# A linear-attention and top-2 mixture-of-experts kernel: ScalarE issues the stores of the rows of x and the early slot fetches, and copies those rows before the logits are summed

## The chip, the cores and the metric

The kernel runs on one core of a Trainium2 chip. The metric is the device time of one execution in microseconds (us). Before the change the median of three runs is 662.22 us (660.88 to 662.79). Below, PE is TensorE's matmul, PEld its weight load, DVE is VectorE, ACT is ScalarE, POOL is GpSimd and SP is SyncE; a q behind a name (SPq) means the engine's sequencer, which waits and issues transfers.

## The reference

```python
# attention: B, H, S, D = 4, 8, 768, 48
f = 1.0 / (1.0 + np.exp(-f_logit))
for t in range(S):
    state = f[:, :, t, :, None] * state + np.einsum('bhd,bhe->bhde', k[:, :, t], v[:, :, t])
    y[:, :, t] = np.einsum('bhd,bhde->bhe', q[:, :, t], state)
# bridge: x = y as rows, (B*S, H*D) = (3072, 384)
# router: E = 8 experts, F = 1024
logits = x @ w_gate
noisy_logits = logits + np.log1p(np.exp(x @ w_noise)) * noise
top2 = np.argpartition(-noisy_logits, 2, axis=1)[:, :2]      # and top2_w: softmax over the two
for e in range(E):
    for k in range(2):
        mask = top2[:, k] == e
        h = np.maximum(x[mask] @ w1[e], 0.0)
        out[mask] += top2_w[mask, k, None] * (h @ w2[e])
```

All of it is float32.

## The kernel before

The sequence is cut into chunks of 128 steps; with 6 chunk positions and 4 batches there are 24 (position, batch) chunks, numbered n = 4c + b. A loop over i runs seven stages, each on another chunk, so that the chunks are pipelined: `forget` on n = i+3 (transposes f, takes its logarithm, line 545 on), `scaled` on i+1 (transposes q and k and scales them on VectorE: qP line 566, kQ line 568), `scores` on i (score matrix, line 580, masked into A, line 583; below the last position also a copy kn on ScalarE, line 576), `summed` on i+2 (running sum L on VectorE, line 554), `output` on i-1 (y, lines 598 and 609, copied to yT on ScalarE, line 613), `decays` on i+2 (P, Q and far on ScalarE, lines 559 to 562) and `features` on i-2. `features` multiplies yT by `w_rt` (line 633), which yields in one PSUM bank the 384 columns of x's rows and the columns of the logits. VectorE sums the logits (`lg`, line 636), then ScalarE copies the rows to `xs` (line 638), and a closure is put in the list `xw` that stores `xs` to `x_rows` in DRAM (line 639). The list is emptied in the next turn of the loop, after the `scaled` stage, that is behind the `forget` instructions of that turn.

PSUM tiles of one bank come from a pool of six banks in rotation, so a bank is written again by the sixth tile after it: the transposes of k in a turn reuse the bank that yT was copied from in the turn before.

After the last chunk of a position, `route` picks two experts for each token, in small pieces between the stages, and queues 8 `puts` (line 710): indirect transfers from POOL that write each token's entry into its expert's list in DRAM (`lists`). Experts are worked on in `items`. The first four items, the early experts, take the first 256 entries of their lists and can start once the first three positions (`HALF`) are routed; their first part is woven into the end of the attention by `first_loads`. Such an item begins with `fetch` (line 815), which reads 256 list entries to `slots`; then `gather` (line 826) on POOL reads the rows of x that the slots name from `x_rows` to `xg`, in two halves; `turned` (line 862) transposes them on TensorE, and the two layers follow (`first_layer`, line 914; `second_layer`, line 1021). Before the change SP issues all plain transfers: the loads of f, q, k and v (line 528), the stores of x, the zeros of out (line 1254), the weights (lines 834 to 844) and the fetches.

Each engine keeps the order in which the program was traced (`in_order`). A transfer is thus issued when its engine comes to it in that order and its semaphores have been reached. In the program as built, the transfers of SP signal their landing on eight semaphores in turn, and each first waits for the transfer that used its semaphore before, the eighth ahead of it.

Of the kernel before, what the change touches and what calls it, by code (L numbers as in the profile page):

```python
# [15 lines left out]
AX = mybir.AxisListType  # L16
ALU = mybir.AluOpType
# [314 lines left out]
def kernel(  # L332
# [38 lines left out]
    nc = tc.nc  # L371
# [4 lines left out]
    C = 128  # L376
# [10 lines left out]
    NE = 4  # L387
# [33 lines left out]
    def one_bank(name):  # L421
        turns.append(turns.pop(0))
        return turns[-1].tile([128, 512], F32, tag="one", name=name)
# [51 lines left out]
    x_rows = tc.dram_tile([N, DM], F32, name="x_rows")  # L475
    lists = tc.dram_tile([LR, 4], U32, name="lists")
# [9 lines left out]
    XW = 2 * D  # L486
# [29 lines left out]
    xw, puts, n_put = [], [], []  # L516
    logf, L, P, Q, qP, kQ, A, kn, yT, lg = ({} for _ in range(10))
# [4 lines left out]
    def cols(hp):  # L522
        return slice(hp * C, (hp + 1) * C)
# [105 lines left out]
    def features(n):  # L629
        c, b = n // B, n % B  # L630
        xp = one_bank(f"xp_{n}")[:, 0:HP * (XW + 2 * E)].rearrange("t (a w) -> t a w", a=HP)
        for hp in range(HP):
            nc.tensor.matmul(xp[:, hp, :], lhsT=yT[n][:, hp % 2, cols(hp // 2)], rhs=w_rt[:, hp, :], start=True, stop=True)  # L633
        if b == 0:
            lg[c] = rt.tile([128, B, 2 * E], F32, tag="lg", name=f"lg_{c}", bufs=NCH)
        nc.vector.tensor_reduce(lg[c][:, b, :], xp[:, :, XW:].rearrange("t a e -> t e a"), axis=AX.X, op=ALU.add)
        xs = wk.tile([128, HP, XW], F32, tag="xs", name=f"xs_{n}", bufs=3)
        nc.scalar.copy(xs, xp[:, :, 0:XW])
        xw.append(lambda: nc.sync.dma_start(out=x_rows[n * C:(n + 1) * C, :], in_=xs.rearrange("t a w -> t (a w)")))


    def route(c):
# [137 lines left out]
    slots, xg, xt, hcol = {}, {}, {}, {}  # L780
# [29 lines left out]
    def fetch(p):  # L810

        assert len(n_put) >= (HALF if p < NE else NCH) * B * 2
        slots[p] = ffn.tile([128, 2, 4], U32, tag=f"slots{p < NE}", name=f"slots{p}", bufs=8)
        row = pairs[p][0] * N + pairs[p][1]
        got = nc.sync.dma_start(out=slots[p], in_=lists[row:row + 256, :].rearrange("(s p) w -> p s w", p=128))
        if p < NE:

            tc.declare_no_dep(got.ins, group="later", reason="slots differ")
            tc.add_to_no_dep_group("full", got.ins)
# [47 lines left out]
    def ahead(what, until):  # L867
        if what in (1, 2):
            most = len(items) if what == 1 else done[1]
        else:  # L870
            most = min(NP if len(n_put) == NCH * B * 2 else NE, NP if what == "fetch" else done["fetch"])
        while done[what] < min(until, most):
            t = done[what]
            done[what] += 1
            fetch(t) if what == "fetch" else gather(t) if what == "gather" else weights(t, what)
# [408 lines left out]
    pieces = chain.from_iterable(((k, i) for i, _ in enumerate(first_layer(k) if k < NE else first_of_two(k))) for k in range(len(items)))  # L1284
    for i in range(-3, NS + 2):
        for stage, lag in ((forget, -3), (scaled, -1), (scores, 0), (summed, -2), (output, 1), (decays, -2), (features, 2)):
            n = i - lag
            if not 0 <= n < NS:
# [26 lines left out]
            for when, first_n, last_n, whose, layer, part in ((output, 13, 16, 0, 1, 0), (output, 17, 18, 0, 2, 0),  # L1315
                                                              (features, 16, 17, 0, 2, 2), (features, 20, 23, 1, 1, 0)):
                if stage is when and first_n <= n <= last_n:
                    part_of_weights(whose, layer, part + n - first_n)
# [14 lines left out]
        n = i - 2  # L1333
        if n >= 0 and n % B == B - 1:
            c = n // B
# [25 lines left out]
    for item, piece in pieces:  # L1361
        p = first_of[item] + max(0, piece - 8) // 7 if item >= NE else item
# [5 lines left out]
        n = item - NE - 2  # L1368
# [52 lines left out]
```

## Time and profile before

| what | value |
|---|---|
| median of 3 runs | 662.22 us |
| the profiled execution's own time | 667.17 us |
| its span on the core | 665.4 us |
| mean granted TensorE clock | 0.985 |
| PE busy | 637.2 us, 96% |
| PEld busy | 550.1 us, 83% |
| DVE busy | 441.8 us, 66% |
| POOL busy | 266.9 us, 40% |
| ACT busy | 254.6 us, 38% |

The profiled execution took 1.77 us more than its span, and 4.95 us more than the median of the unprofiled runs. The times of instructions below are counted from the span's start. Attention takes about the first 170 us, the experts the rest. Matmuls are pipelined and their ends are modelled.

### The profile page before, as it was taken

Reading aid. Unit: us, or ns where it says so; the run is one execution under the profiler, and the core shown is the slowest. Engines: PE = TensorE matmul, PEld = TensorE weight load, DVE = VectorE, ACT = ScalarE, POOL = GpSimd, SP = SyncE. Lnnn points to the kernel's source line nnn. Section 1 sums busy time; section 2 is a strip of 40 time slices with the busy share of each in tenths; the row PEclk is TensorE's granted clock in tenths of the full one; section 3 lists DMA queues with packets and bytes.
Section 4 is the critical chain, followed back from the end, with each engine's and each line's share of the span. In section 5 each row is a group of like instructions: output and inputs, shape, how many; then the busy total and the mean of one; then the engine's idle time right before and its main releaser. Section 6 shows DMA issues by size and latency. Waiting matters only on the chain.

```text
span 665.4 us, 12898 instructions
## 1 busy us (share of the span) xinstructions
PE 637.2 (96%) x4883; PEld 550.1 (83%) x4883; DVE 441.8 (66%) x993; ACT 254.6 (38%) x603; POOL 266.9 (40%) x300
## 2 busy tenths in 40 slices
PE   7999999967999999999999999999999999999991
PEld 7999988856999998999858965995698579889891
DVE  7777867853457666787666676757576667766751
ACT  5876766731221233333233333333322332232320
POOL 7633888715077623261521450325034214413021
PEclk9999999997999999999999999999999999999997
DMA  9999887893599423465725760836184337602112
GB/s 183 190 220 230 187 168 150 186 250 101 168 330 224 106 47 69 118 184 201 222 86 170 170 167 25 292 46 189 26 288 97 91 116 211 180 3 25 22 25 29
DMA packets 153897, 96.31 MB, mean 145 GB/s; under 512 B 115600, under 2 KB 146320, under 8 KB 153824
## 3 DMA queue, kind: packets, MB, share of 16 engines
q1 hardware_dynamic: 141648, 76.12, 41.6%
q0 software_dynamic: 12176, 19.25, 15.3%
q8 instruction: 41, 0.67, 0.4%
q14 instruction: 32, 0.26, 0.1%
HBM read 75.97 MB, written 19.62 MB: 144 GB/s over the span
## 4 chain that ended last, share of the span: by engine, by line
PE 93%; DMA 3%; issue 1%; DVE 1%; POOL 0%; SPq 0%; ACT 0%; POOLq 0%; DVEq 0%
PE y L1021 32%; PE P L939 8%; PE hp L914 6%; PE W L939 5%; PE Z L939 5%; PE V L939 5%; PE X L939 5%; PE xp L633 4%; PE sc L580 4%; PE y L598 4%; PE xgp L862 2%; PE y L609 2%; PE kp L540 2%; PE fp L540 1%; PE qp L540 1%; PE ds L604 1%
## 5 line engine op out<-in xcount | busy, mean ns | idle before, releaser
L1030 POOL DMA_INDIRECT out_dram<-ys,slots x48 | 81.8, 1705 | 154.1 <-ACT ys L1088 131.8
L1021 PE MATMUL y<-qk_all,f_all 128*128 128x192 f32 x576 | 105.2, 327 | 0.0
L1021 PEld LDWEIGHTS y<-qk_all,f_all 128*128 128x128 f32 x576 | 93.3, 190 | 0.3 <-DVE f_all L1003 0.3
L826 POOL DMA_INDIRECT xg<-x_rows,slots x48 | 53.5, 1114 | 50.5 <-DMA slots<-lists 34.1
L1021 PE MATMUL y<-w,hs_b 128*128 128x192 f32 x320 | 59.1, 328 | 0.0
L710 POOL DMA_INDIRECT lists<-entry,sloti x48 | 52.0, 1083 | 10.3 <-issue 9.9
L1021 PEld LDWEIGHTS y<-w,hs_b 128*128 128x128 f32 x320 | 52.9, 190 | 0.9
L1162 POOL DMA_INDIRECT out_dram<-ys_q,slots_q x5 | 8.6, 1718 | 104.0 <-DVE ys_q L1160 104.0
L914 PE MATMUL hp<-xt_a,w 128*128 128x256 f32 x192 | 43.7, 383 | 0.0
L975 ACT ACTIVATE hs_b<-hs_b 128x256 f32<-128x256 f32 (+1 forms) x32 | 15.1, 472 | 71.7 <-DVE hs_b L955 68.4
L914 PEld LDWEIGHTS hp<-xt_a,w 128*128 128x128 f32 x192 | 35.8, 190 | 4.9 <-issue 0.3
L939 PE MATMUL X<-xt_a,w 128*128 128x256 f32 (+1 forms) x128 | 39.7, 432 | 0.0
L939 PE MATMUL Z<-xt_b,v_all 128*128 128x256 f32 (+1 forms) x128 | 39.7, 432 | 0.0
L583 DVE TENSOR_TENSOR A<-sc,causal 128x1024 f32<-128x1024 f32 x24 | 29.3, 1222 | 13.4 <-PE sc L580 7.3
L1088 ACT ACTIVATE ys<-ys,slots 128x384 f32<-128x384 f32 x24 | 14.8, 617 | 59.7 <-DVE ys L1087 49.5
L1080 DVE TENSOR_TENSOR ys<-P,y 128x192 f32<-128x192 f32 x24 | 8.5, 354 | 42.2 <-PE y L1021 29.0
L955 DVE TENSOR_TENSOR hs_b<-hs_a,X 128x256 f32<-128x256 f32 (+1 forms) x32 | 15.6, 487 | 29.9 <-PE X L939 29.8
L1021 PE MATMUL y<-w,f_all 128*128 128x192 f32 x192 | 35.1, 326 | 0.0
L862 PE MATMUL xgp<-ident,xg 128*128 128x128 f32 x144 | 24.3, 279 | 9.9 <-DMA xg<-x_rows,slots 9.9
L939 PEld LDWEIGHTS X<-xt_a,w 128*128 128x128 f32 x128 | 24.3, 190 | 10.1
L939 PEld LDWEIGHTS Z<-xt_b,v_all 128*128 128x128 f32 x128 | 24.3, 190 | 10.1
L955 DVE TENSOR_TENSOR hs_a<-hs_a,P 128x256 f32<-128x256 f32 (+1 forms) x64 | 31.1, 486 | 1.4
(199 smaller groups left out, 1445.1 us busy)
## 6 DMA issues: line engine op xcount, KB each, us to landing
w<-in_moe_w_dram SPq DMA_DIRECT2D x16, 1536.0 KB
w_q<-in_moe_w_dram SPq DMA_DIRECT2D x10, 1536.0 KB
w<-in_moe_w_dram SPq DMA_DIRECT2D x16, 384.0 KB
f_all<-in_f_logit_dram SPq DMA_DIRECT2D x24, 192.0 KB
qk_all<-in_q_dram SPq DMA_DIRECT2D x24, 192.0 KB
qk_all<-in_k_dram SPq DMA_DIRECT2D x24, 192.0 KB
v_all<-in_v_dram SPq DMA_DIRECT2D x24, 192.0 KB
x_rows<-xs SPq DMA_DIRECT2D x24, 192.0 KB
```

The source lines that it names most:

```text
L540: nc.tensor.transpose(p[:, cols(hp)], flat[:, cols(hp)], ident)
L580: nc.tensor.matmul(sc[:, par, cols(hp)], lhsT=kQ[n][rows(par), cols(hp)], rhs=qP[n][rows(par), cols(hp)], start=True, stop=True)
L583: nc.vector.tensor_tensor(A[n].rearrange("j r (a i) -> j (r a) i", i=C), sc.rearrange("j r (a i) -> j (r a) i", i=C), causal.unsqueeze(1). ...
L598: nc.tensor.matmul(at(hp, par), lhsT=vt[:, 2 * hp + par, :], rhs=A[n][:, par, cols(hp)], start=(hp < 2), stop=(c == 0 and hp >= HP - 2))
L710: into = nc.gpsimd.indirect_dma_start(out=lists, out_offset=bass.IndirectOffsetOnAxis(ap=sloti[:, r, b:b + 1], axis=0), in_=entry[:, c, b, ...
L826: nc.gpsimd.indirect_dma_start(out=xg[p][:, s, :], out_offset=None, in_=x_rows[0:HALF * B * C] if p < NE else x_rows, in_offset=bass.Indir ...
L862: nc.tensor.transpose(xp[:, i * 128:(i + 1) * 128], xg[p][:, s, i * 128:(i + 1) * 128], ident)
L914: nc.tensor.matmul(hp[:, o, :], lhsT=w1[home(k)][:, i, (fo + o) * 128:(fo + o + 1) * 128], rhs=xt_a[:, i, k % 2 * 256:(k % 2 + 1) * 256], ...
L939: nc.tensor.matmul(to, lhsT=x, rhs=y, start=start, stop=stop)
L955: nc.vector.tensor_tensor(to, x, y, ALU.add)
L1021: nc.tensor.matmul(P[name], lhsT=x[:, o, :], rhs=y[:, o, :], start=(o == 0), stop=(o == FH - 1))
L1030: into = nc.gpsimd.indirect_dma_start(out=out, out_offset=bass.IndirectOffsetOnAxis(ap=slots[p][:, s, 2:3], axis=0), in_=ys[s], in_offset= ...
```

## The change

Three edits. In `features` the copy of the rows on ScalarE is traced before VectorE's sum of the logits, which reads the same bank. The store of the rows is issued by ScalarE instead of SP. And for the four early items (`p < NE`) the fetch of the slots is issued by ScalarE, not SP.

```diff
@@ features
         if b == 0:
             lg[c] = rt.tile([128, B, 2 * E], F32, tag="lg", name=f"lg_{c}", bufs=NCH)
-        nc.vector.tensor_reduce(lg[c][:, b, :], xp[:, :, XW:].rearrange("t a e -> t e a"), axis=AX.X, op=ALU.add)
         xs = wk.tile([128, HP, XW], F32, tag="xs", name=f"xs_{n}", bufs=3)
         nc.scalar.copy(xs, xp[:, :, 0:XW])
-        xw.append(lambda: nc.sync.dma_start(out=x_rows[n * C:(n + 1) * C, :], in_=xs.rearrange("t a w -> t (a w)")))
+        nc.vector.tensor_reduce(lg[c][:, b, :], xp[:, :, XW:].rearrange("t a e -> t e a"), axis=AX.X, op=ALU.add)
+        xw.append(lambda: nc.scalar.dma_start(out=x_rows[n * C:(n + 1) * C, :], in_=xs.rearrange("t a w -> t (a w)")))
@@ fetch
-        got = nc.sync.dma_start(out=slots[p], in_=lists[row:row + 256, :].rearrange("(s p) w -> p s w", p=128))
+        got = (nc.scalar if p < NE else nc.sync).dma_start(out=slots[p], in_=lists[row:row + 256, :].rearrange("(s p) w -> p s w", p=128))
```

## The prediction

> **What bounds the kernel now.** I read the page first, then TensorE's waits, the chain in order of time, the windows around TensorE's one long wait, and the timelines of SP and ScalarE ahead of it. The page:
>
> ```profile
> PE 637.2 (96%) x4883; PEld 550.1 (83%) x4883; DVE 441.8 (66%) x993; ACT 254.6 (38%) x603; POOL 266.9 (40%) x300
> ...
> PE 93%; DMA 3%; issue 1%; DVE 1%; POOL 0%; SPq 0%; ACT 0%; POOLq 0%; DVEq 0%
> ```
>
> TensorE is the bound: 93% of the chain is its own work, which this change leaves alone. Only the 3% of DMA can be won. TensorE's waits (engine line <- releaser: us in total, times, longest):
>
> ```profile
> PE xgp L862 <- DMA xg<-x_rows,slots: 9.9, 1, 9.9
> PE fp L540 <- DVE f_all L534: 1.8, 2, 1.0
> ```
>
> The chain where it leaves TensorE (start, us, what):
>
> ```profile
> 141.04 1.10 PE sc L580 x16
> 142.23 4.89 DMA slots<-lists
> 147.93 4.85 DMA xg<-x_rows,slots
> 154.50 1.68 PE xp L633 x8
> ```
>
> There is one wait worth naming. TensorE finishes `output` of chunk 21 at 143.75 and goes on at 153.63, when the first gather is there; the gather waited for the slots, whose fetch SP issued only at 142.23. The windows (stretch; width, busy us of PE, PEld, DVE, ACT, POOL; granted clock, DMA share, GB/s) show what follows:
>
> ```profile
> 144.00:150.00 6.00, 0.00 (x0) 0.00 (x0) 0.00 (x0) 0.43 (x2) 1.76 (x2) 0.82 1.06 311
> 150.00:156.00 6.00, 2.37 (x12) 2.40 (x13) 0.56 (x1) 0.00 (x0) 4.81 (x10) 0.50 0.54 159
> 156.00:162.00 6.00, 6.00 (x44) 4.92 (x44) 1.18 (x5) 0.48 (x1) 3.82 (x6) 0.83 0.48 103
> ```
>
> The clock is halved from 147.78, 4.03 after the wait began, to 158.02, 4.39 after it ended. Why was the fetch late? SP's timeline, then ScalarE's:
>
> ```profile
> 135.66 2.23 SPq L639 DMA_DIRECT2D x_rows<-xs  x1
> 137.95 0.43 SPq L528 DMA_DIRECT2D v_all<-in_v_dram  x1
> 138.43 2.73 SPq L844 DMA_DIRECT2D w<-in_moe_w_dram  x2
> 141.25 0.41 SPq L639 DMA_DIRECT2D x_rows<-xs  x1
> ...
> 142.23 0.88 SPq L815 DMA_DIRECT2D slots<-lists  x1
> ```
>
> ```profile
> 130.83 0.50 ACT L638 COPY xs<-xp 128x384 f32<-128x384 f32 x1
> ...
> 132.53 0.20 ACT L549 COPY cap<-f 128x4 f32<-128x4 f32 x1
> 134.46 0.65 ACT L613 COPY yT<-y 128x256 f32<-128x256 f32 x2 [1.73 <-PE y L609]
> ```
>
> SP runs late: the store issued at 141.25 is of chunk 17, whose rows were copied at 130.83. In the order of tracing that store and the fetch stand right behind the `cap` that ends at 132.73, ahead of yT. The last put of the first half was issued by 129.63, so the lists are no hindrance.
>
> **The fetch on ScalarE.** ScalarE reaches it at 132.73, but may not issue it then. The eight landing semaphores are, I take it, dealt over SP's and ScalarE's transfers together, so each waits for the eighth ahead of it. The landings, which the views do not print, I read from the semaphores' updates in the same trace. The store of chunk 17 would wait for the weights issued at 130.25, landed 136.95; the fetch for the q issued at 131.96, landed 138.74. It is then issued at about 138.8, or 3.43 earlier than 142.23. Its flight: 4.89 in the row above; the second fetch (144.18) landed at 147.77, 3.59 later. I take the middle, 4.24, as ScalarE's transfers queue behind fewer of their kind: 0.65 won, ends 0 and 1.3. Then as before 0.81 to the gather, 4.85 flight and 0.85 to the matmul: 138.8 + 4.24 + 0.81 + 4.85 + 0.85 = 149.55 instead of 153.63, 4.08 won. POOL, which does the state of chunk 19 ahead of the gather, is done by about 141.7 then (yT at 139.3, the copy of ds and POOL's 0.73 and 0.62 behind it), so it does not hold it. The other three early fetches lead to gathers that no matmul waited for: 0.
>
> "DMA: Bandwidth & Descriptors" of the Trainium skill (Issuing engines are not separate DMA queues) speaks against more: transfers share the same DMA engines whoever starts them, and a second issuer saves only the time to initiate. By it the flight stays 4.89 and the sum is 3.43; by the row of the second fetch it is 4.73.
>
> **The stores on ScalarE.** SP loses 24 issues; the row of x_rows has their range in ns (least, median, most), and ScalarE's waits have the room for them:
>
> ```profile
> L639 SPq DMA_DIRECT2D x_rows<-xs x24: 319/754/2616, 31.2 to 177.8; - x24
> ```
>
> ```profile
> ACT yT L613 <- PE y L609: 24.9, 17, 2.2
> ```
>
> No ScalarE issue is in the trace. Bounds are 0.32 and 2.62 us; I take the median 0.75, from the same transfer. It cannot be negative, as ScalarE issued nothing before. It stands ahead of kn and yT; behind it all of ScalarE's queue waits (kn, yT, ds, P, Q, far, xs), and for yT TensorE does: yT's second copy ended at 129.54, and the transposes of k that reuse such banks began at 129.98, 0.44 later. ScalarE idles 24.9/17 = 1.46 before yT, so 0.75 is covered, up to 1.46 + 0.44 = 1.90 a chunk. Without that cover the first 18 stores would cost 13.5 us.
>
> The semaphore wait comes on top. For chunks 0 to 12, the eighth transfer ahead landed between 2.86 before and 0.74 after ScalarE came by: covered but for tenths. Chunk 13 is different: ScalarE comes at 107.38, the q issued at 103.52 landed at 112.74, a hold of 5.36. With SP's 0.67 issue of that store, less its own idle 1.68 and 0.44, TensorE gets 3.9 late. Chunks 14, 16 and 17 would be held 4.2 to 4.3, but by then all is 3.9 late, so little comes on top. If the dealing is shifted by one (the k that landed at 114.50), it is 5.6; if SP, relieved of 10.6 us of issue for the stores of chunks 9 to 16, gets its loads landed sooner, it is 0. I take 3.9, the row as it stands. It is nothing at the end while it hides in the wait: TensorE comes to the gather at 143.75 + 3.9 = 147.65, at most 149.35, still before 149.55.
>
> **The rows ahead of the sum.** ScalarE waited for the sum 13.1 us in three waits, 12.05 of them inside TensorE's wait, so 0 is won. Now the sum waits for the copy: for chunk 17 from 129.97 to 131.33, 1.36 later. Behind it on VectorE stand qP (130.38), kQ (130.99), A (131.83) and L. qP moves to about 131.5, 1.1 later; TensorE needs kQ at 136.30 and A (over at 133.06) at 137.40, 4.3 of slack, and the bank of the sum at 132.27, against 131.58 then. Worth 0; where VectorE is full (5.76 of 6 us in 120 to 126) the slack takes the delay. Without it 1.1 a chunk.
>
> **The clock.** TensorE's gap shrinks from 9.9 to 149.55 - 147.65 = 1.9. That is under half of the 4.03 after which the clock fell, so the half-clock stretch of 4.39 goes: at most 2.2 won. But the second half of the gather was issued 2.64 behind the first (150.57, 147.93), and is waited for instead. From the first transposes to the first matmuls of the item (153.63 to 158.44) it took 4.81; now 2.64 + 0.49 for the transposes + 1.09 for the scores = 4.2. Won 0.6, ends 0 and 2.2.
>
> "TensorE: Matmul & The Clock Gate" (Part 1) puts the idle time that halves the clock at about 3.4 us; the trace's gap had lasted 4.03. A new gap between the two would keep this loss by the page, not by the row; mine is under both.
>
> **Sum.** 4.08 + 0.6 = 4.7. From 158 on TensorE is full, and the later loads follow its progress (SP's weights wait 153.7 for W and 121.7 for y), so it stays. The profiled execution's 667.17 becomes 662.5; off the median of 662.22, 4.95 below it, the same gain gives 657.5.
>
> **The rivals.**
>
> *The stall goes altogether.* SP without the stores lands its loads sooner, ScalarE is held by nothing, and the fetch is issued near 133.5. TensorE would be stopped only by its own arrival at 143.75: 9.9 + 0.6 = 10.5 at most, 651.7; halfway, 654. For it: SP's issues are nearly back to back. Against: transfers issued near 131 took 7 us to land, which is not SP's issuing.
>
> *ScalarE becomes the bound of the attention (slower).* Each store holds ScalarE, by issue and semaphore, ahead of yT, and TensorE waits in each chunk. The price is the hold above 1.90; it decides once the lateness of 18 chunks passes 10.5, that is 0.58 a chunk, a mean hold of 2.48. SP's longest issue, 2.62, gives 18 x 0.72 = 13.0, so 2.5 slower: 664.7; with 3.9 more for chunk 13, 668.6. For it: issues of 1.39 to 2.62 for chunks 14 to 16, holds over 4. Against: the median of 0.75, and chunks 0 to 12.
>
> *The fetch is no earlier.* ScalarE, itself late behind stores, comes to it at 142. Then only tenths move: 660.5 to 663.
>
> **How the numbers follow.** Forecast 0.45 (655.5 to 660), the stall gone 0.15, the fetch no earlier 0.12, ScalarE the bound 0.28. About 0.3%, 2 us, is what a measurement of this kernel tells from no change. Faster 0.60 (the first two), same 0.12, slower 0.28. The range leaves out the best of the second case, under 653, and the worst of the last, above 668. The forecast's own range is 655.5 to 660.
>
> **What would show it.** Right: the fetch issued by ScalarE near 139 landing by 143.5; TensorE's wait for xg under 3 us; no half clock after 145; a wait of ScalarE for a DMA before store 13, with yT late and TensorE held some 4 us near 110. Wrong: xp's spacing above 6.5 us from the start (ScalarE binds), a fetch at 133 (stall gone) or after 142, or VectorE's qP late enough that scores wait for it.

## The result

The changed kernel takes 661.92 us (median of 12 runs, 659.16 to 665.33); the kernel before, timed beside it, 661.50 us (12 runs, 658.75 to 662.79). The ratio is 1.0009 [0.9989, 1.0030]: no difference that the measurement can tell. 657.5 and "faster" were forecast. In the comparisons below the medians are of all runs, and the ratio leaves out runs over 1.5% above the fastest of their own kernel: one each in e10 and e11, three each in e6 and e13, and six of 12 in e9, its profiled execution among them.

The profiled execution of the changed kernel seems to tell another story: 662.21 us of its own (span 660.5), 4.96 less than the profiled execution of before, and almost the 662.5 forecast for it. The page after:

```profile
PE 637.2 (96%) x4883; PEld 550.0 (83%) x4883; DVE 441.6 (67%) x993; ACT 254.8 (39%) x603; POOL 271.7 (41%) x300
...
q10 hardware_dynamic: 4544, 4.74, 2.0%
...
PE 87%; DMA 5%; DVE 2%; POOL 1%; ACT 1%; issue 1%; SPq 1%; ACTq 0%; POOLq 0%; DVEq 0%
...
L638 DVE TENSOR_REDUCE lg<-xp 128x16 f32<-128x64 f32 x24 | 5.3, 222 | 42.6 <-ACT xs L637 42.6
```

TensorE's own work is the same 637.2 us, and q10 is ScalarE's new queue. But the chain has lost 6 points of TensorE: it now runs through DMA, VectorE, POOL and ScalarE. Before the sum of the logits VectorE now idles 42.6 us, all of it for the copy xs. TensorE's waits after:

```profile
PE xgp L862 <- DVE sp L658: 1.9, 1, 1.9
...
PE qp L540 <- ACT kn L576: 1.7, 3, 1.0
...
PE y L598 <- ACT yT L613: 0.9, 1, 0.9
```

Of the wait of 9.9 us for the first gather 1.9 is left. The view names VectorE for it, whose `sp` ended at 150.62; but the semaphore for which TensorE's queue had waited just before is that of the gather's second half, which landed at 150.61. Small waits for ScalarE stand where there were none. The windows after (columns as in the prediction):

```profile
144.00:150.00 6.00, 4.24 (x59) 3.53 (x59) 4.26 (x7) 3.21 (x10) 4.93 (x7) 1.00 0.40 100
150.00:156.00 6.00, 5.26 (x29) 4.48 (x30) 4.18 (x13) 0.00 (x0) 4.72 (x9) 0.72 0.26 39
```

TensorE is busy in the stretch that was empty, and the clock is halved for 3.4 us (151.23 to 154.65) instead of 10.2. What it was paid with is in ScalarE's timeline and in the chain in order of time:

```profile
133.64 0.20 ACT L549 COPY cap<-f 128x4 f32<-128x4 f32 x1
138.47 0.33 ACTq L639 DMA_DIRECT2D x_rows<-xs  x1
139.03 0.42 ACTq L815 DMA_DIRECT2D slots<-lists  x1
139.49 0.65 ACT L613 COPY yT<-y 128x256 f32<-128x256 f32 x2 [5.66 <-PE sc L580]
```

```profile
130.65 8.30 DMA out_dram<-zero
...
139.03 0.42 ACTq L815
...
139.49 0.20 ACT yT L613
```

ScalarE stands from 133.84 to 138.47 ahead of the store of chunk 17, and then at the fetch until a zeroing of the output, issued by SP at 130.65, has landed. Nothing in the data asks the fetch to wait for that: the zeroing is the transfer that used the fetch's landing semaphore before. The data alone would not have let it go much sooner here, though: by its semaphore's updates the last put that the fetch reads landed at 138.23. Behind the fetch stands yT, on which the chain goes on. The two profiles are not a fair pair, though: the 667.17 of before lies above all 12 of its runs, the 662.21 of after amid its own. In the runs nothing was won, and the experiments had to show why.

### The profile page after: what moved, and what is told of

It reads as the page before. It is cut to its first block, busy times and chain, and to the rows that moved or that the text cites. A ratio compares the mean times of both kernels' runs of the same rounds, so it can differ in the third digit from the quotient of the medians.

```text
span 660.5 us, 12835 instructions
## 1 busy us (share of the span) xinstructions
PE 637.2 (96%) x4883; PEld 550.0 (83%) x4883; DVE 441.6 (67%) x993; ACT 254.8 (39%) x603; POOL 271.7 (41%) x300
## 4 chain that ended last, share of the span: by engine, by line
PE 87%; DMA 5%; DVE 2%; POOL 1%; ACT 1%; issue 1%; SPq 1%; ACTq 0%; POOLq 0%; DVEq 0%
PE y L1021 32%; PE P L939 8%; PE hp L914 7%; PE X L939 5%; PE V L939 5%; PE Z L939 5%; PE W L939 5%; PE sc L580 3%; PE y L598 3%; PE xp L633 3%; PE xgp L862 2%; DMA f_all<-in_f_logit_dram 1%; DMA out_dram<-zero 1%; PE y L609 1%; PE qp L540 1%; DMA w<-in_moe_w_dram 1%
## 5 line engine op out<-in xcount | busy, mean ns | idle before, releaser
L710 POOL DMA_INDIRECT lists<-entry,sloti x48 | 54.2, 1129 | 11.9 <-issue 9.5
L638 DVE TENSOR_REDUCE lg<-xp 128x16 f32<-128x64 f32 x24 | 5.3, 222 | 42.6 <-ACT xs L637 42.6
L1021 PEld LDWEIGHTS y<-w,f_all 128*128 128x128 f32 x192 | 31.9, 190 | 0.0
```

Source lines behind the costliest of these rows:

```text
L710: into = nc.gpsimd.indirect_dma_start(out=lists, out_offset=bass.IndirectOffsetOnAxis(ap=sloti[:, r, b:b + 1], axis=0), in_=entry[:, c, b, ...
L1021: nc.tensor.matmul(P[name], lhsT=x[:, o, :], rhs=y[:, o, :], start=(o == 0), stop=(o == FH - 1))
```

## The experiments

**Theory H**: the wait for the first gather is real, and the earlier fetch wins what it should; but ScalarE, which now issues transfers, is held at each until an older transfer on the same landing semaphore has landed, and everything behind it (kn, yT, P, Q, xs) is late by that. **Rivals**: the wait of the first profile was an unusual one (A); issuing itself, or the stores' leaving SP's queue, costs the time (T); the new order of copy and sum does (O).

The kernels are made of these edits, on the kernel before:

```diff
W (no wait): the first gather takes given row numbers instead of the fetched slots
+ where = entry[:, 0, s, 0, 0:1] if p == 0 else slots[p][:, s, 0:1]
F (fetches of the early slots):  nc.sync -> nc.scalar or nc.gpsimd, for p < NE
S (stores of the rows of x):     nc.sync -> nc.scalar or nc.gpsimd
O (order): the tensor_reduce to lg stands behind the copy to xs
H (hold alone), in fetch(0):
+ nc.scalar.copy(held, pads["q"][3][0:1, 0, 0:1])
C (close halves), in first_loads:
- ("first", 0, 2), ("second", 0, 1)
+ ("first", 0, 0), ("second", 0, 3)
```

With W the first expert gets other rows than its slots name; all work is done in the same amounts. "Pace" is the time from the first features matmul of chunk 0 to that of chunk 17, read from TensorE's timeline of the profiled execution; "hp" is the start of the first expert matmul there. Medians are us of this kernel / of before on the same chip. e1 to e4 ran on one chip, e5 to e8 on a second, e9 to e15 on a third, e16 and e17 on a fourth. The same change gave 1.0009 and 1.0132 in two sessions, so a difference of ratios from two chips carries a doubt that their intervals do not show.

| run | edits | ratio [interval] | medians | pace | hp |
|---|---|---|---|---|---|
| e1 | none | 0.9992 [0.9966, 1.0017] | 666.84 / 667.19 | 102.5 | 156.27 |
| e2 | W | 0.9860 [0.9815, 0.9905] | 657.89 / 667.19 | 103.9 | 147.50 |
| e3 | W, change whole | 0.9995 [0.9971, 1.0018] | 668.40 / 667.19 | 115.1 | 161.22 |
| e4 | F ScalarE | 0.9994 [0.9967, 1.0022] | 666.94 / 667.19 | 103.8 | 157.26 |
| e5 | F POOL | 0.9937 [0.9908, 0.9966] | 665.68 / 669.59 | 104.3 | 153.38 |
| e6 | W, S ScalarE | 1.0011 [0.9976, 1.0047] | 673.55 / 669.59 | 108.5 | 163.55 |
| e7 | W, O | 0.9917 [0.9885, 0.9950] | 663.81 / 669.59 | 103.3 | 153.03 |
| e8 | change whole | 1.0132 [1.0085, 1.0179] | 678.22 / 669.59 | 111.4 | 164.71 |
| e9 | S ScalarE | 0.9994 [0.9962, 1.0026] | 674.88 / 670.34 | 115.5 | 162.58 |
| e10 | W, S POOL | 0.9827 [0.9792, 0.9862] | 660.50 / 670.34 | 103.0 | 150.31 |
| e11 | W, F ScalarE | 1.0003 [0.9976, 1.0030] | 670.67 / 670.34 | 105.0 | 153.79 |
| e12 | F POOL, C | 0.9896 [0.9862, 0.9931] | 663.45 / 670.34 | 104.1 | 153.03 |
| e13 | W, H | 0.9964 [0.9928, 1.0000] | 669.74 / 671.21 | 104.6 | 159.73 |
| e14 | F and S POOL, C | 0.9844 [0.9806, 0.9883] | 659.62 / 671.21 | 103.0 | 153.78 |
| e15 | F and S POOL, O | 0.9928 [0.9901, 0.9955] | 665.64 / 671.21 | 107.1 | 158.67 |
| e16 | F and S POOL | 0.9857 [0.9817, 0.9897] | 662.24 / 670.89 | 102.9 | 154.61 |
| e17 | F and S POOL, O, C | 0.9872 [0.9834, 0.9910] | 663.15 / 670.89 | 104.4 | 154.39 |

**The wait is real: e1 and e2.**

> The kernel of before once more, unchanged, for a second profile and to see how far two timings of one program differ. Theory A (the first profile caught an unusually long wait of TensorE for the first gather; the timed executions have a shorter one): the profiled execution's own time comes nearer 662 than 667, with the wait for xg at 3 to 7 us instead of 9.9; timed 1.000. Theory B (the wait is 9.9 us in every execution and the changed kernel lost as much elsewhere): 667 and 9.9 us again; timed 1.000.

> Before, with the first early expert's gather taking its row numbers from a constant tile instead of the fetched slots, so that it need not wait for the fetch; it gathers other rows than the reference's, as many of them. SP still issues the fetch. Theory A: TensorE's wait for xg in the timed executions is worth some 5 us, so 0.990 to 0.997. Theory B: the whole 9.9 and 0.6 for the clock go, 0.984 (651 us). If it is 1.000, the timed executions of before have no such wait at all.

A second profile of the unchanged kernel before has the wait again (9.07 us) and 10.2 us at half clock; rival A falls. Without the wait the kernel is 0.0140 x 667.19 = 9.3 us faster, and nothing else of size stands in TensorE's waits of e2:

```profile
PE kp L540 <- DMA qk_all<-in_k_dram: 1.2, 1, 1.2
PE xgp L863 <- DMA xg<-x_rows,entry: 0.8, 1, 0.8
```

**The change without the wait: e3, and the change again: e8.**

> The changed kernel with the same constant row numbers for the first gather (other rows than the reference's). Its profile showed TensorE waiting 1.9 us for xg's second half. Theory A: little is left of the wait for the fetch, 0.995 to 1.000 of before, and slower than before without the wait, as ScalarE's stores still make TensorE late in the attention (by about 2.6 us at chunk 19 in the profile). Theory B: the same as before without the wait.

> The changed kernel once more, unchanged, beside the others on one chip, and for a second profile. Theory S: 0.998 to 1.002; its profile shows ScalarE held ahead of some of the stores of chunks 7 to 17 by other amounts than the first profile's (2.4, 3.0, 1.1, 0.9, 1.6, 2.7, 0, 0.5, 4.6 us for chunks 9 to 17), and the first matmul of the first expert nearer to before's 156 to 158 us than to 153. If it is 0.990 to 0.995, the first timing was the odd one.

With the wait taken away, the change costs all that this had brought: from 0.9860 to 0.9995, 9.0 us. ScalarE's timeline in e3, then SP's, then the line of TensorE's waits:

```profile
81.64 0.20 ACT L549 COPY cap<-f 128x4 f32<-128x4 f32 x1
89.44 0.33 ACTq L639 DMA_DIRECT2D x_rows<-xs  x1
89.81 0.58 ACT L576 COPY kn<-kp 128x512 f32<-128x512 f32 x1 [7.97 <-DMA f_all<-in_f_logit_dram]
```

```profile
83.39 0.74 SPq L528 DMA_DIRECT2D f_all<-in_f_logit_dram  x1
```

```profile
PE fp L540 <- ACT kn L576: 5.4, 1, 5.4
```

ScalarE is ready for a store at 81.84. The load of f for which it is held is issued by SP only at 83.39; by its semaphore's updates it lands at 89.42, and the store goes at 89.44. So ScalarE waits not only for a landing but for SP to get there: ScalarE does no work for 7.97 us ahead of kn, and TensorE stops for 5.41. In all, ScalarE is held some 25 us ahead of stores 7 to 17 in e3, 22 in e8, and 17 in the profile after; the pace is 115.1, 111.4 and 105.5 us. How much is lost differs by execution. In e8 the change was 1.3% slower than before. TensorE's waits there:

```profile
PE qp L540 <- ACT kn L576: 3.9, 3, 2.0
PE fp L540 <- ACT kn L576: 2.6, 1, 2.6
```

Not all of the difference lies in the attention. From hp to the end the profiled times leave 508.2 to 509.0 us in before, after and e1 to e4, and 510.8 to 512.7 in e5 to e7, on e8's chip; but 514.4 in e8, where TensorE once waits 2.5 us (at 213.7, for `xt_a`) and runs at half clock for 3.4 us, and 518.1 in e9. What makes this part longer, no run shows.

**The fetch alone on ScalarE, with and without the wait: e4 and e11.**

> Of the change only the four fetches on ScalarE; the stores stay on SP and the sum of the logits ahead of the copy. Theory A: ScalarE issues the fetch when its semaphore is free, near 139, and no store holds ScalarE before, so TensorE is not late in the attention: 0.993 to 0.999, faster than the changed kernel. Theory B: no gain beyond the changed kernel's, 1.000.

> Gather 0 by constant row numbers as in e2, and the fetches are issued by ScalarE; stores and order as before. The fetch is useless to the first gather, so only its cost on ScalarE is seen. Theory H: ScalarE is held at the fetch till 139 to 141, the copy yT of chunk 19 waits behind it, as in e4 (140.33 instead of 133.22), TensorE stops for 2 to 3 us there and runs at half clock for 3.4 us: 4 us more than e2, ratio 0.989 to 0.994. Rival: the hold is swallowed by the slack of the last chunks, ratio 0.984 to 0.988 as e2.

In e4 ScalarE issues the fetch at 139.86, against SP's 140.41 in e1: 0.55 earlier. ScalarE's timeline:

```profile
139.86 0.43 ACTq L815 DMA_DIRECT2D slots<-lists  x1
140.33 0.65 ACT L613 COPY yT<-y 128x256 f32<-128x256 f32 x2 [6.46 <-DMA qk_all<-in_q_dram]
```

ScalarE's `cap` had ended at 133.87. The fetch is held for the last load of q, and yT is held with it. TensorE waits 2.7 us for that yT, 4.4 for xg, and hp starts at 157.26, no earlier than in e1. So the fetch alone, without a store on ScalarE and in the old order, wins nothing. In e11, where the first gather does not need the fetch, the same hold costs 1.0003 - 0.9860 = 1.4%, 9.5 us, more than the 4 us that I expected. The two ran on different chips; on e11's own chip the other version without the wait, e10, has 0.9827.

**The hold without a transfer: e13.**

> As e2 (gather 0 by constant row numbers, fetches and stores on SP), with one thing more: where the fetch of slot 0 stands in the program, ScalarE copies one number of chunk 23's q load, the transfer for which ScalarE waited ahead of its fetch in e11 (landed 137.86 there, 139.21 in e2). ScalarE issues no transfer at all. Theory H (the price of a transfer on ScalarE is the hold until an older transfer lands, not its issuing): ScalarE stands 4 to 7 us ahead of the copy yT of chunk 19, and the loss of e11 against e2 comes back: ratio 0.993 to 1.002. Rival (issuing on ScalarE's queue, or SP's running on past the fetch, makes the loss): as e2, 0.983 to 0.988.

```profile
140.25 0.19 ACT L817 COPY held<-qk_all 1x1 f32<-1x1 f32 x1 [6.78 <-DMA qk_all<-in_q_dram]
140.35 0.62 ACT L614 COPY yT<-y 128x256 f32<-128x256 f32 x2
```

ScalarE issues nothing here and copies one number from that load of q. This alone brings back 1.04% of the 1.43% of e11. The intervals of e11 and e13 overlap, so that of the rest nothing is shown. The loss falls on the same place: yT at 140.35, TensorE stopped for 2.55 us at 138.21, two stretches at half clock (3.4 and 10.2 us), hp at 159.73. So the larger part of the fetch's price is the hold and not the issuing.

**The stores: e6, e9 and e10.**

> Before with the constant row numbers for the first gather (other rows than the reference's), and of the change only the stores on ScalarE. The reference point is before without the wait, 0.986. Theory S: the stores hold ScalarE on a semaphore for several us around chunks 9 to 17 and TensorE comes late by as much; most of the 10.5 us between the two kernels without the wait is theirs: 0.995 to 1.000. Theory O (the later sum of the logits is what makes TensorE late): 0.986 to 0.989.

> Only the stores of the rows of x go to ScalarE; the fetches stay on SP, the sum stays ahead of the copy, the wait for the first gather stays. Theory H (ScalarE is held at its stores by landing semaphores that it shares with SP's loads, as the sum of holds of 17 to 25 us in the four kernels with such stores): holds of 15 to 25 us again in stores 7 to 17, TensorE late by 6 to 14 us in the attention, part of it swallowed by the wait that is still there (9 to 10 us in all): ratio 1.008, range 1.000 to 1.020. Rival C (what was lost came from the fetch on ScalarE or from the new order, or from two of them together): no lateness, ratio 0.997 to 1.002.

> Gather 0 by constant row numbers as in e2 (so no wait for the first fetch), and the stores are issued by POOL instead of ScalarE or SP; all else as before. Theory H: what costs is that ScalarE is held, and ScalarE issues no transfer here, so the chunks keep their pace: as e2 (0.986) with at most 24 x 0.8 us of issuing on POOL, which is 1% busy: ratio 0.984 to 0.992. Rival T (it is the stores' leaving SP's queue that costs: SP runs on to other loads, the traffic falls otherwise): as e6, ratio 0.997 to 1.005.

Stores on ScalarE cost 1.0011 - 0.9860 = 1.5% where there is no wait to hide them (e6, holds of 21.6 us in sum); on e6's own chip e7, which has the new order instead of the stores, has 0.9917. The same stores on POOL cost nothing (e10, 0.9827), though they leave SP's queue just the same and POOL is busy for 40% of the span in before, not the 1% of the expectation: rival T falls. With the wait in place (e9) the ratio is 0.9994, but from only half of its widely spread runs; by all 12 the median is 0.7% above that of before. As long as the attention is late by less than the wait, the wait swallows it. Pace tells the lateness apart from the wait: the five executions with stores on ScalarE (the profile after, e3, e6, e8, e9) have 105.5 to 115.5 us, those without them and in the old order 102.5 to 105.0, and 104.1 the profile of before.

**The order of copy and sum: e7, e15, e16, e17.**

> Before with the constant row numbers for the first gather (other rows than the reference's), and of the change only the copy ahead of the sum. Theory S: the sum's wait of 1.1 to 1.4 us a chunk is inside VectorE's slack of some 4 us: 0.985 to 0.988, as before without the wait. Theory O: 0.993 or more.

> The changed kernel whole, new order included, with POOL in ScalarE's place for the fetches and the stores, and the halves of the first gather as far apart as before. Theory H: what the change lost, it lost by ScalarE's holds, so it gains now what it was meant to: as e5 (0.9937) or better by what the stores' leaving SP gives, 0.986 to 0.994; the new order costs up to 3.8 us of it (e7 against e2). Rival O (the new order is at fault for a good part): 0.996 to 1.002.

> Fetches and stores on POOL as in e14 and e15, the sum ahead of the copy as before, the halves of the first gather as far apart as before: e15 without the new order, e14 without the closer halves. Theory O (the sum, put behind the copy xs, holds VectorE for as long as ScalarE is late, as the 4.31 us at 116.09 in e15): without the order 3 to 5 us less than e15 (0.9928): ratio 0.985 to 0.989. Rival (the difference between e14 and e15 is the closer halves): 0.991 to 0.995.

> e14 with the new order of copy and sum, nothing else changed. Theory O: 3 to 5 us more than e14 (0.9844): ratio 0.988 to 0.993. Rival (the closer halves made the difference between e14 and e15): as e14, 0.982 to 0.987.

Three pairs differ in O alone: e7 over e2 0.57%, e15 over e16 0.71%, e17 over e14 0.28%. All point the same way, and only e15 and e16 have intervals that do not touch; their mean is 0.5%, some 3.5 us. Each pair is from two chips. Within a chip, e15 is 0.84% above e14 and e17 0.15% above e16; C stands in e14 and e17 alone, so that it cancels in the mean of the two, which is 0.5% again, if the shares of O and C add up. e7 and e17 lie between the ranges of their two theories, so the size stays uncertain. e15 shows how (ScalarE's timeline, then VectorE's):

```profile
114.45 0.63 ACT L559 ACTIVATE P<-L 128x512 f32<-128x512 f32 x1 [3.91 <-POOL st L626]
```

```profile
116.09 0.23 DVE L638 TENSOR_REDUCE lg<-xp 128x16 f32<-128x64 f32 x1 [4.31 <-ACT xs L637]
```

ScalarE's P waits 3.91 us for POOL's state. In the old order VectorE need not wait for xs to sum the logits and go on; now the sum stands behind xs, xs behind P, and `lack`, qP, kQ and A behind the sum. TensorE waited 2.3 us for `lack`. The new order passes such a lateness of ScalarE on to VectorE.

**Versions that beat the kernel before: e5, e12, e14.**

> Before, with the four early fetches issued by POOL, whose transfers signal on semaphores of their own; stores on SP and the sum ahead of the copy as in before. Theory S (what keeps an early fetch from going out is the turn of the eight shared semaphores, on SP or on ScalarE, and not the lists): the fetch goes out near 132 to 134, the gather near 138, TensorE's wait for xg goes from 9 us to under 2 and the clock stays full: 0.984 to 0.988, like before without the wait. Theory D (the list's entries, or the transfers in flight, set the time): the fetch lands no sooner than 143, 0.995 or more.

> The kernel before with the fetches of the early slots on POOL (as e5), and the second half of the first gather traced straight behind its first half, with the two turns of pause behind both. In e5 a put of 0.99 us stood between the halves (142.58) and TensorE waited 1.43 us more for the second one: that wait goes to 0.2 or so, 1.2 us less than e5: ratio 0.992 (0.989 to 0.995). Rival: the put that now stands behind the second half makes something else as late, ratio 0.9937 as e5 or above.

> Correct version: fetches of the early slots and all stores of the rows of x on POOL, the halves of the first gather side by side as in e12, the sum ahead of the copy as before. Theory H: as e12 (0.9896) with what e10 gave against e2 (0.9827 to 0.986): the fetch waits a little for POOL at 135, the wait for xg stays at 1 to 3 us, no chunk late in the attention: ratio 0.984 to 0.990. Rival (POOL becomes the late engine: 24 stores and 4 fetches of 0.6 to 0.8 us, and the gather behind the store of a late chunk): 0.990 to 0.998.

POOL's transfers signal on eight other semaphores (111 to 118 in the traces; SP's and ScalarE's use 101 and 103 to 109), so they are not held by SP's loads. In e5 it issues the fetch at 135.22, 5.2 earlier than SP in e1, and the kernel wins 0.63%, 4.2 us. That lies between the ranges of theories S and D: the turn of the shared semaphores had held the fetch, but the lists hold it too. The last put that it reads landed at 134.63, and TensorE still waits 5.0 us for the gather. With the stores on POOL too and the two halves of the gather side by side it wins 1.56% [1.17, 1.94], 10.5 us (e14). The size of the share that C has is open: e12 over e5 gives 0.4%, e14 over e16 0.1%, with intervals that overlap. POOL's timeline of e14, then the line of TensorE's waits:

```profile
137.68 0.76 POOL L815 DMA_DIRECT2D slots<-lists  x1 [1.85 <-DMA lists<-entry,sloti]
...
141.95 1.04 POOL L826 DMA_INDIRECT xg<-x_rows,slots  x1 [0.15 <-issue]
```

```profile
PE xgp L862 <- DMA xg<-x_rows,slots: 4.4, 1, 4.4
```

The fetch waits only for a put, as its data ask (the last that it reads was issued at 131.81 and landed at 137.39), and less than half of the old wait is left.

## Why the prediction was wrong

Two steps failed. The fetch on ScalarE was to win 4.08 us, with no price for what is held behind it; moved alone (e4) it won nothing (0.9994 [0.9967, 1.0022]). The holds at the stores were to be one of 5.36 us and to hide; they were 17 to 25 us in sum. The first alone is enough to undo the forecast. What the second takes with the wait in place is 0 to 0.7% by e9, whose runs spread.

**The bound and the wait: right.** One wait of TensorE, with the half clock behind it, was all there was to win: 9.3 us by e2, 10.5 at most by the prediction.

**The fetch on ScalarE: right instants, partly by luck, and the main cost left out.** 139.03 was measured for 138.8, a flight of 4.15 for 4.24, 0.85 to the gather for 0.81, and hp at 153.20 for 149.55 + 4.2 = 153.75. But the eighth transfer ahead was not the one that the order of tracing gives. The semaphores in the trace of after are dealt over both queues, but with SP's transfers further ahead: the fetch waited for the zeroing, which is traced behind it, and not for q. Nor are the lists "no hindrance": the last put was issued by 129.63, but landed at 133.93 in before and at 138.23 in after. The gather's own flight was put at 4.85 and was 3.09 (144.03 to 147.12), so that its first half was not waited for at all. And the term of 3.43 was read from one late execution: in e4 against e1 the fetch is 0.55 earlier. The prediction did write "yT at 139.3", but gave that hold no price in the sum; e11 and e13 price it at 1.0 to 1.4%, 7 to 9.5 us, where no wait hides it. "DMA: Bandwidth & Descriptors" of the Trainium skill (Issuing engines are not separate DMA queues), which the prediction weighed, says that a second issuer saves only the time to initiate. The runs do not speak against it: the flight was 4.15 and 5.15 us on ScalarE in the profile after and in e4, and 4.89 and 5.26 on SP in before and in e1.

**The stores on ScalarE: the holds were sized far too small.** Each term of it can be read now. The issue was put at 0.75; in the profile after it is 0.33 (0.33 to 0.47). The cover of 1.90 was about right in the one place where I read it: in e3 a wait of ScalarE of 7.97 stopped TensorE for 5.41, a cover of 2.6. The holds were put at one of 5.36, with chunks 0 to 12 covered, by the landings of the eighth transfer ahead in the order of tracing. Measured were holds ahead of most stores from chunk 7 or 9 on, 17 to 25 us in sum, as the transfer waited for is a later one that SP may not even have issued. TensorE's lateness of 3.9 became 1.4 to 11.5 us (paces of 105.5 to 115.5 against 104.1 in the profile of before). That it hides in the wait was right in kind: without the wait the stores cost 1.5% (e6), with it 0.9994 or, by all runs, 0.7% (e9).

**The rows ahead of the sum: wrong.** They were put at 0, with 4.3 us of slack on VectorE. That slack was read in a turn in which ScalarE was on time; once ScalarE waits, the sum waits with it, and so does VectorE. Measured 0.3 to 0.7% by three pairs, each from two chips.

**The clock: a rule that failed.** The gap was put at 1.9 us and was 1.94 (148.80 to 150.74), by luck, since it was the wait for the gather's second half and not for its first. That such a gap keeps the full clock, as it is under half of 4.03, was wrong: a stretch of 3.4 us at half clock followed.

**The sum and the median.** The gain of 4.7 held between the two profiled executions (4.96), not between medians. The execution profiled before, 667.17, lay above every timed run beside it, while the profiled one of after, 662.21, lies at its median of 661.92. The forecast for that execution was met, 662.5, by luck, as two of its terms failed; the one for the median was not. To carry a difference between two single executions over to the median was a step of its own, and it failed.

**The rivals.** "ScalarE becomes the bound of the attention" named what happened: holds above the cover, ahead of kn and yT. Its condition was wrong: it asked for a mean hold of 2.48 over 18 chunks, while 17 to 25 over 18 is a mean of 0.9 to 1.4; a few holds of 4 to 8 us are enough, as the cover of a chunk isn't saved up for another. Its price of 2.5 to 6.4 us was passed in e8 (8.6 us slower); in the first session the change was neither faster nor slower. "The stall goes altogether", at most 10.5 us, is what POOL as issuer of both comes to (e14, 10.5). "The fetch is no earlier", with 660.5 to 663 us, holds the 661.92 that was measured, and e4 without the stores bears it out, but by another road: ScalarE was held for a landing, not late behind its stores.

## What to carry to other kernels

In a program built like this one, a transfer moved to an engine that computes brings a wait along: until the transfer before it on the same landing semaphore has landed, and that one may belong to another queue and not be issued yet. Price the hold for all that stands behind it on that engine, not for the transfer alone, and look first for an engine whose queue doesn't share those semaphores; here POOL won 1.4 to 1.6% (e16, e14) with the transfers that won nothing on ScalarE. Where a long wait stands behind a stage, it hides what that stage loses: take the wait away in an experiment before you call a cost zero.

## What the hardware showed that was not expected

- The same store takes the issuing engine 0.33 us on ScalarE (at most 0.61, in e3), 0.60 on POOL (e14) and a median of 0.75 on SP in before, up to 4.92 in e11. SP's least is 0.32, so its long issues do not belong to the transfer; what makes them long, no run shows.
- Half-clock stretches last 3.4, 6.8 or 10.2 us in all profiles, but for the last one, which runs past the end of the program. "TensorE: Matmul & The Clock Gate" of the Trainium skill (Part 1) has a free-running window of 3.413 us, which agrees. It asks for an idle window of about 3.4 us ahead of it; here a gap of 1.71 us (e9, at 117.84) or 1.94 (profile after) was followed by 3.4 us at half clock, while one of 2.60 (e8, at 88.4) was not. So by these rows a shorter gap than the page's can be enough; what else it takes, no run shows.
- The same program was 0.1% slower than the kernel before in one session and 1.3% in another. The holds differ from one execution to the next (17 us in the profile after, 22 in e8), but part of the loss in e8 lies behind hp, so they are not shown to be all of it.
